# A flag over the softmax sums of a decode kernel, and a branch at the end to a second form of the layers

## The chip, the cores and the metric

The kernel runs on one core of one Trainium2 chip. The metric is the device time of one launch in microseconds (us), less is better. Every run is one whole launch: four decode layers, from the inputs in HBM to the output in HBM. The profile comes from one execution of its own, with its own time beside its span.

## What is computed

A token step for 8 batch rows (`x` is 8 x 1 x 448) passes through attention, mixer and MLP, and then through the same two again with the same weights and the same caches:

```python
def _A_ref(x, k_cache, v_cache, wq, wo):
    q = (x @ wq).reshape(B, 1, 16, 256).transpose(0, 2, 1, 3)
    k = jnp.repeat(k_cache, 2, axis=1)      # caches: 8 x 8 x 4096 x 256 bf16
    v = jnp.repeat(v_cache, 2, axis=1)
    p = softmax(einsum("bhqd,bhkd->bhqk", q, k) * 256 ** -0.5)
    return einsum("bhqk,bhkd->bhqd", p, v).transpose(0, 2, 1, 3).reshape(B, 1, 4096) @ wo

x = x + _A_ref(layernorm(x), k_cache, v_cache, wq, wo)
x = x + _B_ref(layernorm(x), w1, w2, w3, w4)     # twice, A then B
```

The sequence has one token, so the shifted groups of the mixer inside `_B_ref` are zero, and the kernel computes of B only the inner norm and the MLP (448 to 1792 to 448, tanh gelu). The softmax of the reference subtracts the row's maximum; the kernel takes exp of the scaled scores as they are, sums them, and divides at the end.

## The kernel before, in words

The keys and the values are 134 MB each over all rows, far more than the on-chip memory, so they stream. The work is cut into units of one pass (0 or 1, for the two attention layers), one batch row and one pair of key heads (`gp`, 4 of them). A unit has four chunks of K and four of V, of 1 MB each. Python lists fix the order by hand: `items` is the order of use, `loads` the order of the transfers, and `emit_loads` (L948) puts a load on SP's queue as soon as one of 17 places of 8,192 bytes per partition (`places`, L80) is given up by its last reader. Part of each row's K and V stays on the chip between the two passes. All transfers of the caches go through SP's one queue, and a waiting load holds up those behind it.

For a K chunk DVE turns 32 x 32 blocks (`transpose_k`, L1017), PE forms the scores (L1036), and ACT takes exp with a running sum (`exps`, L1044), whose sums land in `zall`. PE turns the weights p (L1087), ACT spreads them (L1286), and PE multiplies them with V (L1104, or L1120 for the last row).

`z_cols` (L521) runs 55 times, once for each group of units that is finished: DVE adds the two partial sums into `zs` (L527), spreads them over four columns (L530), PE adds over the partitions with a matrix of ones (L538), and DVE takes the reciprocal into `rz` (L541). `zs`, `zm` and `rz` have one buffer each. The instructions of such side work are generators, stepped between the chunks (`step`, L1190), so their place in every engine's queue is fixed when the program is built.

GpSimd (POOL) does little: it makes the identity matrix, and raises variances to the power -0.5 (L304 and, in the tail, L1572).

The tail begins with the last V chunks (L1120 and L462 in turn), and goes on with the sum over wo, the double norm (L1530 to L1576), the MLP (L1581, L1606, L1614, L1630), the last addition (L1639) and four small transfers of the output, two from SP and two from ACT (L1641). Behind them stands the end of the program (all under L1669): every engine goes on into the block that follows; SP waits for the eight DMA semaphores and the engines' counters, and two rounds of a barrier of all five engines close the run.

Small constants (`usel`, `parity`, `wv`, `one`, `eps2`, `nhalf`) are tiles of their own, behind `places` in the same pool.

Of the kernel before, what the change touches and what calls it, by code (L numbers as in the profile page):

```python
# [8 lines left out]
FP32 = mybir.dt.float32  # L9
BF16 = mybir.dt.bfloat16  # L10
U32 = mybir.dt.uint32
ACT = mybir.ActivationFunctionType
ALU = mybir.AluOpType
EPS = 1e-5


@with_exitstack
def kernel(
# [12 lines left out]
    out: bass.AP,  # L31
):

    nc = tc.nc
    Bn, Sq, D = A_x.shape
    G = A_k_cache.shape[1]
# [2 lines left out]
    HD = A_wq.shape[1]  # L51
# [43 lines left out]
    identb = consts.tile([128, 128], BF16, name="identb")  # L95
    nc.vector.tensor_copy(identb[:], ident)

    usel = consts.tile([128, 4], FP32, name="usel")
    for u in range(2):
        nc.vector.tensor_reduce(  # L100
            usel[:, 2 * u : 2 * u + 2],
# [2 lines left out]
            ALU.add,  # L104
        )

    parity = consts.tile([128, 2], FP32, name="parity")
    nc.vector.tensor_reduce(
        parity[:], ident.rearrange("p (m k) -> p k m", k=2), mybir.AxisListType.X, ALU.add
    )  # L110
    xq = consts.tile([128, 2, Bn], BF16, name="xq")

# [35 lines left out]
        at, n = {"y": (0, 8), "st": (64, 2)}[what]  # L148
        return store[0][:, at : at + n * nb]

    wv = consts.tile([128, 4], FP32, name="wv")
    nc.vector.memset(wv[:, 0:3], 1.0 / D)
    nc.vector.memset(wv[0:64, 3:4], 0.0)
    nc.vector.memset(wv[64:128, 3:4], 1.0 / D)
    one = consts.tile([128, 1], FP32, name="one")
    nc.vector.memset(one[:], 1.0)
    ones = one[:].to_broadcast([128, 128])
    HTw = consts.tile([128, HC, Bn], BF16, name="HTw")
    nc.vector.memset(HTw[:], 0.0)
    low = consts.tile([128, 2, 4], FP32, name="low")  # L160
    for k, v in enumerate((1.0, (1 + EPS) ** -0.5)):
        nc.vector.memset(low[:, k], v)
        nc.vector.memset(low[0:64, k, 3:4], 0.0)
    eps2 = consts.tile([128, 2], FP32, name="eps2")
    nc.vector.memset(eps2[:, 0:1], EPS)
    nc.vector.memset(eps2[:, 1:2], EPS * EPS / (1 + EPS))
    nhalf = consts.tile([128, 1], FP32, name="nhalf")
    nc.vector.memset(nhalf[:], -0.5)
    xb = {}
    for nb in (1, Bn):  # L170
        xb[nb] = consts.tile([128, 5, nb], BF16, name=f"xb{nb}")
# [72 lines left out]
    def norm(x, nb, twice, xe=None):  # L244

        xe = xbs(nb) if xe is None else xe

        def room(name, shape, at):  # L250
            n = shape[0] * shape[1]
            if nb < Bn:
                t = chn.tile([128, n * MID], FP32, tag=name)
                ap = t[:, 0 : n * nb]
            else:
                ap = scratch(at, n * nb)
            return ap.rearrange("p (s f b) -> p s f b", s=shape[0], f=shape[1])

        def bc(ap):
            return ap.unsqueeze(1).to_broadcast([128, 4, nb])  # L260

        xx = room("xx", (2, 4), 0)
        nc.vector.tensor_mul(xx[:, 0], x, wv[:].unsqueeze(2).to_broadcast([128, 4, nb]))
        nc.vector.tensor_mul(xx[:, 1], xx[:, 0], x)
        mv = room("mv", (1, 2), 528)[:, 0]
        if nb == 1:
            yield 3
            st = room_ps("st", 1)
            nc.tensor.matmul(
                st, ones, xx.rearrange("p s f b -> p (s f b)"), start=True, stop=True  # L270
            )
            yield 0
            nc.vector.tensor_reduce(
                mv[:, :, 0],
                st.rearrange("p (s f) -> p s f", s=2),
                mybir.AxisListType.X,
                ALU.add,
            )
        else:
            xs = room("xs", (1, 2), 512)[:, 0]  # L280
            nc.vector.tensor_reduce(
                xs, xx.rearrange("p s f b -> p s b f"), mybir.AxisListType.X, ALU.add
            )
            yield 3
            st = room_ps("st", nb)[:, 0 : 2 * nb].rearrange("p (s b) -> p s b", b=nb)
            nc.tensor.matmul(st, ones, xs, start=True, stop=True)
            yield 0
            nc.vector.tensor_copy(mv, st)
        var = room("var", (1, 1), 608)[:, 0, 0]
        if nb == 1:  # L290
            nc.vector.scalar_tensor_tensor(
                var, mv[:, 0], mv[:, 0], mv[:, 1], ALU.mult, ALU.subtract, reverse1=True
            )
        else:
            nc.vector.tensor_mul(var, mv[:, 0], mv[:, 0])
            nc.vector.tensor_sub(var, mv[:, 1], var)


        ve = room("ve", (1, 2), 544)[:, 0]
        n = 2 if twice else 1  # L300
        rs = room("rs", (1, 2), 560)[:, 0]

        def power(k0, k1):
            nc.gpsimd.tensor_tensor(  # L304
                rs[:, k0:k1].rearrange("p n b -> p (n b)"),
                ve[:, k0:k1].rearrange("p n b -> p (n b)"),
                nhalf[:].to_broadcast([128, (k1 - k0) * nb]),
                ALU.pow,
            )

        if twice and nb == 1:
            nc.vector.scalar_tensor_tensor(
                ve[:, :, 0], var.to_broadcast([128, 2]), 0.0, eps2[:], ALU.max, ALU.add
            )
            power(0, 2)
        else:
            if twice:
                nc.vector.tensor_scalar(
                    ve[:, 1], var, 0.0, EPS * EPS / (1 + EPS), ALU.max, ALU.add
                )  # L320
                power(1, 2)
            nc.vector.tensor_scalar(ve[:, 0], var, 0.0, EPS, ALU.max, ALU.add)
            power(0, 1)
        xc = room("xc", (1, 4), 576)[:, 0]
        nc.vector.tensor_tensor(xc, x, bc(mv[:, 0]), ALU.subtract)  # L325
        yield 0
        if nb > 1:
            yield
        c = (1 + EPS) ** -0.5 if twice else 1.0
        rl = rs[:, n - 1]  # L330
        parts = ((0, 128, 0, 0, 3, 0), (0, 64, 64, 3, 4, 4), (64, 128, 64, 3, 4, 3))
        if nb == 1:
            nc.vector.scalar_tensor_tensor(
                xe[:, 0:4, 0], xc[:, :, 0], rl, low[:, int(twice)], ALU.mult, ALU.mult
            )
            parts = parts[1:2]
        for p0, p1, x0, f0, f1, to in parts:
            pp = slice(x0, x0 + p1 - p0)
            dst = xe[p0:p1, to : to + f1 - f0, :]
            if nb == 1:  # L340
                nc.vector.tensor_scalar(dst, xc[pp, f0:f1], rl[pp], c, ALU.mult, ALU.mult)
            else:
                nc.vector.scalar_tensor_tensor(
                    dst,
                    xc[pp, f0:f1],
                    c,
                    rl[pp].unsqueeze(1).to_broadcast([p1 - p0, f1 - f0, nb]),
                    ALU.mult,
                    ALU.mult,
                )  # L350
        if twice and nb == 1:
            nc.vector.scalar_tensor_tensor(x, xc, rs[:, 0], x, ALU.mult, ALU.add)
        elif twice:
            nc.vector.tensor_tensor(xc, xc, bc(rs[:, 0]), ALU.mult)
            nc.vector.tensor_add(x, x, xc)
        yield 2
# [36 lines left out]
    def tail_cols(r0, r1, ps, two):  # L393

        nb = r1 - r0
        nc.vector.tensor_copy(
            two.rearrange("p (r k) -> p r k", k=2),
            identb[:, 64:128].unsqueeze(2).to_broadcast([128, 64, 2]),
        )
        nc.tensor.matmul(ps, two, xb[Bn][:, 3, r0:r1], start=True, stop=True)  # L400
        nc.vector.tensor_tensor(
            xq[:, :, 0:nb],
            ps.unsqueeze(1).to_broadcast([128, 2, nb]),
            parity[:].unsqueeze(2).to_broadcast([128, 2, nb]),
            ALU.mult,
        )
        return lambda xi: xb[Bn][:, xi, r0:r1] if xi < 3 else xq[:, xi - 3, 0:nb]
# [109 lines left out]
    def mlp(b0, nb):  # L517
        HT = yield from mlp_hidden(b0, nb)
        yield from out_cols(lambda c: HT[:, c, :], w4_of, range(HC), b0, nb, 2)

    def z_cols(zall, gps):  # L521

        np_ = len(gps)
        zm = chn.tile([128, 4, np_], FP32, tag=f"zm{np_}")
        zs_t = chn.tile([128, 2], FP32, tag="zs")
# [4 lines left out]
        nc.vector.tensor_tensor(  # L530
            zm[:],
            zs.unsqueeze(1).to_broadcast([128, 4, np_]),
            usel[:].unsqueeze(2).to_broadcast([128, 4, np_]),
            ALU.mult,
        )
        yield
# [2 lines left out]
        yield 0  # L539
        rz = chn.tile([128, 4, np_], FP32, tag=f"rz{np_}")  # L540
        nc.vector.reciprocal(rz[:], z_ps)  # L541
        return rz

    def scale_o(o_ps, rz, gp, u, OT):
# [746 lines left out]
    for idx, it in enumerate(items):  # L1291
        if idx == len(items) - 2:
# [6 lines left out]
            x_ps = store[1][:, 0:W]  # L1299
            nc.vector.memset(x_ps, 0.0)  # L1300
            nc.scalar.activation(end[1][:, W : W + 1], identb[:, 0:1], ACT.Gelu_apprx_tanh)
        n, kv, c = it
        ps, b, gp = tasks[n]
        if idx in o_late_at:
# [235 lines left out]
        return ap.unsqueeze(1).to_broadcast([ap.shape[0], n, nb])  # L1540

    xx = temp(8 * nb).rearrange("p (s f b) -> p s f b", s=2, f=4)
    nc.vector.tensor_mul(xx[:, 0], xs, wv[:].unsqueeze(2).to_broadcast([128, 4, nb]))
    nc.vector.tensor_mul(xx[:, 1], xx[:, 0], xs)
    m_ps = store[4][:, 256 : 256 + 8 * nb]
    nc.tensor.matmul(m_ps, ones, xx.rearrange("p s f b -> p (s f b)"), start=True, stop=True)
# [23 lines left out]
    nc.vector.tensor_scalar(ve[:, 0:nb], var, 0.0, EPS, ALU.max, ALU.add)  # L1570
    for k in (nb, 0):
        nc.gpsimd.tensor_tensor(  # L1572
            rs[:, k : k + nb], ve[:, k : k + nb], nhalf[:].to_broadcast([128, nb]), ALU.pow
        )
    centre(xe[0:64, 4:5, :], 64, 128, 3, 4)
    centre(xe[64:128, 3:4, :], 64, 128, 3, 4)  # L1576
# [66 lines left out]
        )  # L1643


# [1 line left out]
_INS = ['A_x', 'A_k_cache', 'A_v_cache', 'A_wq', 'A_wo', 'B_x', 'B_w1', 'B_w2', 'B_w3', 'B_w4']  # L1647
_OUTS = [((8, 1, 448), 'bfloat16')]
# [25 lines left out]
```

## Time and profile before

| | us |
|---|---|
| median of three runs | 1033.33 (1033.24 to 1033.99) |
| profiled execution, its own time | 1033.59 |
| its span (first to last instruction) | 1031.4 |
| outside the span | 2.2 |

| engine | busy us | share of the span | instructions |
|---|---|---|---|
| PE, matmul | 660.3 | 64% | 12706 |
| DVE | 585.0 | 57% | 1211 |
| ACT | 213.1 | 21% | 688 |
| POOL | 16.3 | 2% | 27 |
| SP's DMA queue, of 16 DMA engines | | 99.2% | 67840 packets, 419.66 MB |

How to read it: the span is one execution from its first instruction to the last barrier. A line such as L541 is a line of the kernel before; in the changed kernel the same statement has a higher number. "Idle before" is the time an engine stood still ahead of a group, and the name behind the arrow says who ended it. SPq, ACTq and so on are the engines' instruction queues, in which a DMA is issued. The part on the DMA queues counts what the 16 transfer engines did; q8 and q14 there carry the program itself to the engines.

### The profile page before, as it was taken

To read this page: it belongs to the slowest core of one execution; us is meant where nothing else is said; L and a number is where in the kernel's file an instruction comes from. 1 tells how busy PE (TensorE), PEld (TensorE's weight loads), DVE (VectorE), ACT (ScalarE), POOL (GpSimd) and SP (SyncE) were. 2 spreads that over 40 slices of the span, in tenths; PEclk is the share of its full clock that TensorE was granted. 3 is DMA by queue.
4 is the path that set the end of the run, shared out by engine and by line. 5 is a ranking of instruction groups with operands and counts; after the bars stand their busy time and mean duration, and the time that the engine had idled before them with its cause. 6 is when DMAs were issued, how large, how long until landed. Compare 5 with 4: busy or idle time off the path is not lost.

```text
span 1031.4 us, 28604 instructions
## 1 busy us (share of the span) xinstructions
PE 660.3 (64%) x12706; PEld 419.0 (41%) x12706; DVE 585.0 (57%) x1211; ACT 213.1 (21%) x688; POOL 16.3 (2%) x27
## 2 busy tenths in 40 slices
PE   2154545776578558765875587567765775577775
PEld 2032323453245335533553355334533453345545
DVE  6344577259725971596259725882497159625581
ACT  1011111141214120411141214121422041214120
POOL 0000000000000000000000000000000000000000
PEclk9965555565665665755565656556656575666655
DMA  9999999999999999999999999999999999999995
GB/s 377 394 428 420 422 425 418 401 409 424 415 404 423 423 415 402 414 424 414 397 418 422 417 406 418 423 417 401 415 424 414 407 412 425 417 395 419 416 421 209
DMA packets 68010, 421.48 MB, mean 409 GB/s; under 512 B 7080, under 2 KB 11952, under 8 KB 42288
## 3 DMA queue, kind: packets, MB, share of 16 engines
q1 hardware_dynamic: 67840, 419.66, 99.2%
q8 instruction: 99, 1.62, 0.6%
q14 instruction: 23, 0.19, 0.1%
q10 hardware_dynamic: 48, 0.01, 0.0%
HBM read 419.63 MB, written 0.01 MB: 407 GB/s over the span
## 4 chain that ended last, share of the span: by engine, by line
DMA 51%; DVE 22%; PE 20%; issue 3%; ACT 2%; SPq 1%; POOL 0%; DVEq 0%; ACTq 0%
DMA places<-in_A_v_cache_dram 35%; DVE places L1021 18%; DMA places<-in_A_k_cache_dram 14%; PE sc L1036 8%; PE o L1104 5%; PE misc L601 2%; PE misc L180 2%; DMA w_sb<-in_B_w_dram 1%; DVE qbd L424 1%; ACT p_n L1045 1%; PE misc L538 1%; SPq L199 1%; DVE store L1067 1%; PE misc L462 1%; PE misc L1087 1%
## 5 line engine op out<-in xcount | busy, mean ns | idle before, releaser
L1021 DVE STREAM_TRANSPOSE places<-places 128x512 uint32<-128x512 uint32 (+2 forms) x384 | 443.7, 1212 | 43.2 <-DMA places<-in_A_k_cache_dram 42.9
L1104 PE MATMUL o<-places,ptw 128*8 128x256 bf16 x3808 | 247.4, 383 | 141.7 <-DMA places<-in_A_v_cache_dram 113.1
L1036 PE MATMUL sc<-places,qbd 128*8 128x256 bf16 (+1 forms) x4736 | 234.5, 354 | 145.4 <-DVE places L1021 143.0
L1036 PEld LDWEIGHTS <-qbd 128*8 128x8 bf16 x4736 | 123.2, 105 | 211.4 <-DVE places L1021 122.7
L1104 PEld LDWEIGHTS <-ptw 128*8 128x8 bf16 x3968 | 102.9, 101 | 207.7 <-issue 130.4
L1045 ACT ACTIVATE p_n<-sc 128x256 bf16<-128x256 f32 x128 | 95.5, 746 | 326.8 <-PE sc L1036 323.3
L1286 ACT COPY ptw<-psv 128x32 bf16<-128x32 bf16 x248 | 52.9, 228 | 179.3 <-PE o L1104 177.5
L424 DVE CAST qbd<-misc 32x16 bf16<-32x16 f32 (+1 forms) x184 | 30.8, 168 | 62.2 <-PE misc L418 60.4
L601 PE MATMUL misc<-R_t,o_t 128*128 128x4 f32 (+1 forms) x212 | 46.3, 325 | 27.7 <-DVE qbd L424 11.3
L601 PEld LDWEIGHTS misc<-R_t,o_t 128*128 128x128 f32 x212 | 42.1, 276 | 44.4 <-issue 18.1
L1094 ACT CAST psv<-misc 128x128 bf16<-128x128 f32 x64 | 17.0, 266 | 196.3 <-PE misc L1087 196.3
L541 DVE RECIPROCAL rz<-misc 128x4 f32<-128x4 f32 (+1 forms) x55 | 9.4, 172 | 82.2 <-PE misc L538 37.9
L1072 ACT COPY places<-store 128x1024 bf16<-128x1024 bf16 x40 | 40.2, 1028 | 11.2 <-PE o L1104 10.9
L538 PE MATMUL misc<-zm,one 128*128 128x4 f32 (+1 forms) x110 | 28.3, 328 | 18.2 <-DVE zm L530 15.8
L538 PEld LDWEIGHTS misc<-zm,one 128*128 128x128 f32 x110 | 23.5, 266 | 33.7 <-DVE zm L530 22.1
L180 PEld LDWEIGHTS <-w_sb 128*128 128x128 bf16 x896 | 27.7, 105 | 16.5 <-issue 16.5
L1045 ACT ACTIVATION_READ_ACCUMULATOR p_n<-sc 128x1 f32 x128 | 34.0, 266 | 0.0
L555 ACT COPY o_t<-o 128x256 f32<-128x256 f32 x53 | 19.7, 372 | 58.2 <-PE o L1104 58.2
L304 POOL TENSOR_TENSOR t<-t,nhalf 128x2 f32<-128x2 f32 (+2 forms) x18 | 12.0, 669 | 951.4 <-DVE t L325 951.4
L1067 DVE TENSOR_SCALAR store<-places 128x512 uint32<-128x512 uint32 x40 | 24.8, 673 | 0.0
L1087 PEld LDWEIGHTS <-p_n 128*128 128x128 bf16 x256 | 11.5, 105 | 30.2 <-issue 19.3
L605 DVE CAST qT<-misc 128x8 bf16<-128x8 f32 (+1 forms) x37 | 7.2, 195 | 27.8 <-PE misc L601 20.1
(157 smaller groups left out, 370.7 us busy)
## 6 DMA issues: line engine op xcount, KB each, us to landing
places<-in_A_k_cache_dram SPq DMA_DIRECT2D x79, 2048.0 KB, 15.3
places<-in_A_v_cache_dram SPq DMA_DIRECT2D x193, 512.0 KB, 7.1
places<-in_A_v_cache_dram SPq DMA_DIRECT2D x87, 1024.0 KB, 19.5
places<-in_A_k_cache_dram SPq DMA_DIRECT2D x34, 1024.0 KB, 12.0
rest<-in_A_v_cache_dram SPq DMA_DIRECT2D x8, 640.0 KB, 16.3
places<-in_A_wq_dram SPq DMA_DIRECT2D x5, 768.0 KB, 12.8
places<-in_A_v_cache_dram SPq DMA_DIRECT2D x8, 384.0 KB, 15.7
wo_sb<-in_A_wo_dram SPq DMA_DIRECT2D x1, 2688.0 KB, 19.7
```

Of the source, the lines that this page charges most:

```text
L180: nc.tensor.matmul(bass.AP(out.tensor, out.offset, [out.ap[0], (1, WIDE)]), w, x.to_broadcast([128, WIDE]), start=start, stop=stop, skip_g ...
L424: nc.vector.tensor_copy(qbd[32 * a : 32 * a + 32, :, g0 : g0 + ng, a, :], qs.rearrange("p e (f g u h) -> p (e f) u g h", f=2, u=2, h=2)[:, ...
L538: nc.tensor.matmul(z_ps, ones, zm[:], start=True, stop=True)
L601: nc.tensor.matmul(ot_ps[:, j], o_sb[:].rearrange("p (i j) -> p j i", j=2)[:, j], R, start=True, stop=True)
L1021: nc.vector.transpose(w, w)
L1036: nc.tensor.matmul(sc[32 * k : 32 * k + 8, 128 * (x % 2) : 128 * (x % 2 + nx)], qbd[:, ep, gp % 2].rearrange("p a h -> p (a h)"), v, start ...
L1045: nc.scalar.activation(p_sb[:, :, :, 2 * u : 2 * u + 2].rearrange("p t i x -> p x t i"), sc[:, 0:256].rearrange("p (x t i) -> p x t i", x= ...
L1067: nc.vector.tensor_single_scalar(kept_words.bitcast(U32), words.bitcast(U32), 0, op=ALU.bitwise_or)
L1072: nc.scalar.copy(words, kept_words.bitcast(BF16))
L1087: nc.tensor.matmul(pt_ps[:, t], p_sb[:, t].rearrange("p i x -> p (i x)"), cols, start=True, stop=True,)
L1104: nc.tensor.matmul(o_ps[32 * q : 32 * q + 8, :], ptz[:, at : at + 8], v[:, y * Dh : (y + 1) * Dh] if v2 is None or y < PR else v2[:, (y - ...
L1286: nc.scalar.copy(ptw[:, ring_of[it], :, 6:8], psv[slot_of[it[0]]][:, it[2]])
```

## The change

The old body becomes a function `layers_unshifted`. Each call of `z_cols` now adds its reciprocals and its sums into a tile `seen` on POOL: two additions per call, 110 in all. Before the last item of the list the sums of `seen` are added over the partitions (one matmul with ones), copied by ACT, added up by DVE and compared with 1e12: `bad` is 1 where the total is larger or not a number. At the end each engine loads `bad` into a register and branches. Where `bad` is 0, the engine goes on through a short block to the end; where it is 1, it runs `layers_shifted`, a second, plain form of all four layers, which subtracts the maximum ahead of exp and writes the output again. The second form stands in the program between the branch and the end.

In the built program this gives each engine a register load and a compare-and-branch behind its last instruction (SP's register load stands ahead of its two output transfers). In the short block for `bad` = 0 every engine waits for its own counter and raises it by what the other way would have added; SP does so for the eight DMA semaphores, one wait each, and then all jump over the second form: over 17,619 instructions on PE, 1,910 on DVE, 522 on SP, 275 on ACT and 21 on POOL, of 64 bytes each. In the closing block SP has eight waits instead of five ahead of the barriers. In the first form the engines' instructions keep their order; what is new among them are POOL's additions, the four instructions of the flag, and a wait for POOL at the addition into `zs` on DVE, since POOL must have read the last `zs`.

The small constants become parts of one tile `few`, and `seen` and `bad` are placed first. In the lists of tile addresses of the two built programs `places` begins at byte 16,512 of each partition before and at byte 16,608 after (remainders by 64: 0 and 32; by 256: 128 and 224), `rest` moves likewise, and the kept weights go the other way: `wq_sb` from 163,616 to 163,584 (remainders by 64: 32 and 0), and `w3_sb`, `wo_sb` and `w4_sb` with it.

```diff
+SAFE = 1e12
...
+    flags = ctx.enter_context(tc.tile_pool(name="flags", bufs=1))
+    seen = flags.tile([128, 12], FP32, name="seen")
+    bad = flags.tile([128, 1], mybir.dt.int32, name="bad")
+    layers_unshifted(tc, seen[:], bad[:], A_x, ..., out)
+    flag = tc.nc.values_load(bad[0:1, 0:1], min_val=0, max_val=1)
+    with tc.If(flag > 0, preferred_fallthrough_block=False):
+        layers_shifted(tc, A_x, ..., out)
...
+    few = consts.tile([128, 16], FP32, name="few")
+    def small(n):
+        ...
+        return few[:, at : at + n]
+    nc.gpsimd.memset(seen, 0.0)
-    usel = consts.tile([128, 4], FP32, name="usel")
+    usel = small(4)
...
     def z_cols(zall, gps):
...
         rz = chn.tile([128, 4, np_], FP32, tag=f"rz{np_}")
         nc.vector.reciprocal(rz[:], z_ps)
+        for e, part in (
+            (seen[:, 0 : 4 * np_], rz[:].rearrange("p n g -> p (n g)")),
+            (seen[:, 8 : 8 + np_], zs),
+        ):
+            nc.gpsimd.tensor_tensor(e, e, part, ALU.add)
         return rz
...
+        if idx == len(items) - 1:
+            seen_ps = store[4][:, 0:2]
+            nc.tensor.matmul(seen_ps, ones, seen[:, 8:10], start=True, stop=True)
+            nc.scalar.copy(seen[:, 8:10], seen_ps)
+            nc.vector.tensor_reduce(
+                seen[:, 10:11], seen[:, 0:10], mybir.AxisListType.X, ALU.add
+            )
+            nc.vector.tensor_scalar(bad, seen[:, 10:11], SAFE, 0.0, ALU.is_le, ALU.is_equal)
...
+def layers_shifted(ctx, tc, A_x, ..., out):
+    for _ in range(2):
...
+        for b in range(Bn):
+            for g in range(G):
+                kt = work.tile([128, NS, Dh], BF16, name="kt")
+                nc.sync.dma_start(kt[:], A_k_cache[b, g].rearrange("(p n) d -> p n d", p=128))
+                vt = work.tile([128, NS, Dh], BF16, name="vt")
+                nc.sync.dma_start(vt[:], A_v_cache[b, g].rearrange("(p n) d -> p n d", p=128))
...
+                    nc.scalar.activation(p[:, h], s[:, h], ACT.Exp, bias=down[:, h : h + 1],
+                                         accum_out=z[:, h : h + 1])
...
+    nc.sync.dma_start(out.rearrange("b s d -> (b s) d"), rows[:])
```

## The prediction

> **What bounds the kernel now.** I read the page's DMA rows first, then the end of the chain of waits and the timeline there, then SP's waits, then the packet records of the trace, then POOL's rows.
>
> ```profile
> DMA  9999999999999999999999999999999999999995
> GB/s 377 394 428 420 422 425 418 401 409 424 415 404 423 423 415 402 414 424 414 397 418 422 417 406 418 423 417 401 415 424 414 407 412 425 417 395 419 416 421 209
> ...
> q1 hardware_dynamic: 67840, 419.66, 99.2%
> q8 instruction: 99, 1.62, 0.6%
> q14 instruction: 23, 0.19, 0.1%
> ```
>
> The 16 transfer engines are busy from the first slice to the last but one: the bytes on SP's queue are the bound, not an engine. In the packet records a packet of the caches takes about 8 ns plus 0.0369 ns per byte (medians 159 ns for 4,096 bytes, 312 for 8,192, 613 for 16,384). Summed by that line, the packets make 1,001 us of the 1,021 us up to the last V packet. The missing 20 us are hiccups of less than a microsecond.
>
> The chain of waits at the end, and the timeline of its last lines:
>
> ```profile
> 1006.18 15.25 DMA places<-in_A_v_cache_dram
> 1021.42 0.05 issue
> 1021.47 0.39 PE store L1120 x8
> 1021.86 0.02 issue
> 1021.88 0.18 DVE qT L548
> ...
> 1028.29 0.27 DVE places L1639
> ```
>
> ```profile
> 1028.29 0.27 DVE L1639 TENSOR_TENSOR places<-places,store 128x112 bf16<-128x112 f32 x1
> 1028.59 0.71 SPq L1641 DMA_DIRECT2D out_dram<-places  x2
> 1028.60 0.65 ACTq L1641 DMA_DIRECT2D out_dram<-places  x2
> ```
>
> From 1021.4 on nothing is transferred: one chain of small steps runs to 1028.56, then the output goes out. SP's waits in that window:
>
> ```profile
> SPq L1641 <- DVE places L1639: 17.4, 1, 17.4
> SPq L1669 <- DMA out_dram<-places: 1.1, 1, 1.1
> SPq L1669 <- PEq L1669: 0.6, 2, 0.4
> ```
>
> SP's issue ends at 1029.30; 1.1 us later, at 1030.40, the output has landed. The other 1.04 us to 1031.44 are SP's further waits (each starts 0.065 us after the one before) and the two barriers. So two places count: the stream, where only what reaches the transfers costs, and the 10 us after it, where everything on the chain costs in full.
>
> **The change part by part.**
>
> *In the stream.* POOL gets 110 additions of 128x1 to 128x8. No plain addition on POOL is in the trace; the nearest rows:
>
> ```profile
> L304 POOL TENSOR_TENSOR t<-t,nhalf 128x2 f32<-128x2 f32 x8 | 5.6, 701 | 824.3 <-DVE t L325 824.3
> L304 POOL TENSOR_TENSOR t<-t,nhalf 128x1 f32<-128x1 f32 x8 | 4.4, 551 | 78.8 <-DVE t L325 78.8
> L304 POOL TENSOR_TENSOR t<-t,nhalf 128x4 f32<-128x4 f32 x2 | 2.0, 1012 | 48.3 <-DVE t L325 48.3
> ...
> L1658 POOL MEMSET const-float32-0.0<- 128x1 f32 x1 | 0.1, 98 | 0.2 <-issue 0.2
> ```
>
> A power is the dearest thing POOL does here, a fill the cheapest, so one addition costs between 0.1 and 0.55 (one column) or 1.0 us (four); by 55 pairs that is 11 to 85 us on an engine busy for 16.3 of 1031. Behind POOL's queue stand only its own powers: each starts 6.4 us or more after the reciprocal ahead of it, and a pair needs at most 1.7 us with its hand-overs of 0.05 to 0.07. Cost nothing.
>
> DVE's addition into `zs` now waits until POOL has read the last `zs`. In the trace it follows the previous reciprocal by 1.01 to 1.45 us eleven times and by 4.06 us or more otherwise. A pair at 0.3 us each is done in 0.7, a pair of powers in 1.7; so it waits 0 to 0.7 us, eleven times at most, 0 to 7 us on DVE. Queued behind it are the transposes (L1021), for which PE's scores wait, and through the places SP's loads. I take nothing: the loads are 7 to 20 us from issue to landing, and the transfer engines stay at 1.01 in the densest DVE stretch (217 to 250 us, DVE busy 27.4 of 33). If that cover is gone, the few hiccups near these waits (0.6 us at 207, 0.2 at 412) say about 0.3 us for each of eight places: up to 2.4 us.
>
> Could POOL slow DVE by reading on-chip memory at the same time? At 969.03 three transposes ran beside two powers with two inputs each, and took 1235, 667 and 668 ns; without POOL the same forms take 1180 to 1240 and 660 to 680. Nothing.
>
> *In the tail.* The matmul with ones (and its loads) stands on PE between two V chunks. Row: L538 at 1014.86 took 0.57 us. PE finishes the chunk ahead at 1019.95 and starts the next at 1020.19, when it lands; now it starts near 1020.6, and its two pieces end near 1021.6, where the last 8 matmuls would have begun at 1021.47. Bounds 0 and 0.4; I take **0.2**, since the last piece still waits for its transfer. ACT's copy (idle until 1026.46) and DVE's two instructions (about 0.15 each) end near 1021.4, ahead of DVE's next step at 1021.88; hidden, and 0.3 us if that half microsecond of cover is gone. SP's register load waits for them with 7 us until the output.
>
> *At the end.* In the order of SP: the output lands at 1030.40 + 0.2. Eight waits in the short block instead of the first of five: the three for the output end with the landing, six more at 0.065 make 0.4, the branch 0.05. Then the jump, F. Then eight waits in the closing block, where four were left: 0.26 more. Together **0.7 + F**. ACT comes beside it: its issue ends at 1029.25, a register load (not in the trace; between 0.05 for an instruction that the sequencer does alone and the 2.1 us that the load of x takes from issue at 0.73 to its use at 2.85) ends by 1031.35, so at worst it adds 0.5. Nothing taken.
>
> F is the largest term. In the trace each branch goes to the next block, and DVE enters the closing block about 0.05 us after its last instruction is handed over. Now the target lies 522 x 64 = 33,408 bytes ahead on SP and 1.13 MB on PE. The program comes in packets: 99 of 16,384 bytes on q8, which is PE's 24,945 instructions of 64 bytes in order, and 23 of 8,192 bytes on q14 for the others. They come one block after the other in order, so the target cannot be there and has to be fetched while the engine stands. Price from rows: issue to first packet, as for the output (1028.59 to 1029.38), 0.79; the packet, 1.06 on q8 and 0.32 on q14; last packet to the wait's end (1029.80 to 1030.40), 0.60. That is 1.7 us for SP's block and 2.45 for PE's. PE is there by 1028.2 plus a register load of at most 2.1, so it ends near 1032.8, much like SP at 1032.7. Lower bound 0.05, upper bound two such fetches in series, 4.9. I take **2.45**, the dearer of the two single fetches, since the barrier waits for the last of five engines.
>
> [...]
>
> *Start.* POOL's clearing of `seen` is one more 0.1 us beside a stream that SP starts at 0.73; `few` changes no count. Nothing.
>
> Sum: 0.2 + 0.7 + 2.45 = 3.35 us on the execution of 1033.59, which lies 0.26 above the median shown; on the median **1036.7 us**, 0.32% slower.
>
> **The rivals.**
>
> *The jump is cheap* (not slower than a measurement tells). If the target is at hand, or the engines fetch it while SP waits for the landing, F is 0.05 and the end costs 0.2 + 0.75: **1034.3**. For it: PE, DVE and ACT do wait up to 2 us for SP in any case, and the fetch packets are short. Against it: SP itself jumps after the landing. It decides if F stays under 1.2 us.
>
> *The places lie worse.* `places` moves from remainder 0 by 64 bytes to 32. In the packet records, without those held up by over 12%, 4,096-byte packets of wq took 163.8 ns into `wq_sb` (remainder 32), V's of that size 161.5 into `places` (remainder 0); 1,792-byte ones 78.5 into the kept weights, 76.1 into `places`. If these 2.4 ns belong to the address, some 57,300 packets of the stream pay them on 16 engines: 8.6 us, less 0.5 for 3,456 packets of weights that get better: 8.1 more, **1044.8**. Against it: the 896-byte packets go to remainder 32 as well and have a median of 41.0, exactly the line, and the first packets into `wo_sb` take 74, the line too; a toll of the address would spare none. So the difference looks like crowding in that stretch.
>
> [...]
>
> *POOL reaches the transfers* through the wait on `zs`: 2.4 more, **1039.1**.
>
> *The change does something else:* the flag comes out as 1, and the second form runs. Its caches alone, 537 MB at 409 GB/s, are 1,313 us more, over **2340**. The sums are of some 4,096 terms near 1 for each head, the total far from 1e12.
>
> **How the numbers follow.** Forecast (1035.4 to 1039) 0.58; cheap jump 0.14; places worse 0.17, at the second price 0.03; POOL 0.06; second form 0.01; anything faster 0.01. A measurement of this kernel tells about 0.2%, 2.1 us, from no change. Faster 0.01, same 0.14, slower 0.85. The range goes from just under the cheap jump, 1034.2, to just over the first price of the address, 1045; outside are the second price, the second form and little else.
>
> **What would show it.** In the changed profile: the first output packet 0.2 us later, and between the landing and the span's end some 4.2 us instead of 1.04, with instruction packets in them; cache packets at the same 159, 312 and 613 ns and 99% busy; rows of POOL's additions under 0.5 us, and no wait for POOL ahead of L1021. I am wrong if the gap behind the landing stays under 2 us (F), if the medians of the packets move by 2 ns or more (address), or if SP's waits for DVE grow (POOL).

## The result, and the profile after

| | before | after |
|---|---|---|
| median | 1033.53 us (1033.24 to 1034.45) | 1041.07 us (1039.20 to 1042.13, six runs) |
| profiled execution, its own time | 1033.59 | 1039.20 |
| its span | 1031.44 | 1037.41 |

The changed kernel is slower: ratio 1.0069, 95% interval 1.0056 to 1.0082. It costs 7.5 us where 3.35 were forecast. The time lies in the range, 4.4 us above the forecast; it lies above the 1035.4 to 1039 that the forecast itself stood for, and the range reaches so far only because it was drawn out to the rival of the address. The profiled execution happens to be the fastest of the six, so its parts add up to 5.6 us and not to 7.5.

The page of the changed kernel, DMA rows:

```profile
DMA  9999999999999999999999999999999999999993
GB/s 381 410 425 420 420 423 415 399 423 423 412 400 425 425 409 391 414 424 411 402 417 425 411 403 420 424 412 392 424 422 406 402 417 423 411 392 414 419 419 148
...
q1 hardware_dynamic: 67840, 419.66, 98.7%
q8 instruction: 101, 1.65, 0.6%
q14 instruction: 31, 0.25, 0.1%
```

SP's queue carries the same 419.66 MB, so the second form did not run. The program comes in 2 packets more on q8 and 8 more on q14. Two and six of them come behind 1031 us, when the engines jump; the other two on q14 also come in `watch_only` and `near` below, which have no far jump. The last slice has fallen from 209 to 148 GB/s, since it holds more time without transfers.

Its chain of waits at the end (start, us, what):

```profile
1007.63 15.86 DMA places<-in_A_v_cache_dram
1023.49 0.05 issue
1023.53 0.39 PE store L1153 x8
1023.92 0.02 issue
1023.95 0.18 DVE qT L581
...
1030.43 0.27 DVE places L1681
```

The steps shown are those of before, 2.1 us later from 1023.49 on. Its timeline, first at the new matmul, then at the output:

```profile
1021.80 0.56 PE L1338 MATMUL store<-seen,few 128*128 128x2 f32 x2
1022.21 0.51 PEld L1153 LDWEIGHTS <-places 128*128 128x128 bf16 x16
1022.22 1.03 PE L1153 MATMUL store<-psv,places 128*128 128x2 bf16 x24
...
1023.53 0.38 PE L1153 MATMUL store<-psv,places 128*128 128x2 bf16 x8 [0.28 <-DMA places<-in_A_v_cache_dram]
...
1030.73 0.70 SPq L1683 DMA_DIRECT2D out_dram<-places  x2
1030.73 0.65 ACTq L1683 DMA_DIRECT2D out_dram<-places  x2
```

Ahead of its last 8 matmuls PE still waits 0.28 us for the last piece of V (0.26 before), so the new matmul delays nothing there. SP's waits behind 1020 us (total, times, longest):

```profile
SPq L39 <- DVE bad L1343: 15.0, 1, 15.0
SPq L1683 <- DVE places L1681: 6.9, 1, 6.9
SPq L40 <- SPq L40: 1.3, 3, 0.7
SPq L1892 <- PEq L1892: 0.6, 2, 0.4
```

SP waits 15 us for the flag (L39), but the output needs 6.9 more: hidden. The three waits of L40 are the output's landing. Between them and L1892, the closing block, no row shows anything: the branch instructions are counted in no view, so that gap has to be read from the sequencer's records in the trace. There SP's last branch starts at 1033.23 and its next instruction at 1036.08.

Cut into four stretches that join, both profiled executions read so (last packet of the weights, last packet of V, first issue of the output, end of the span):

| us | before | after | difference |
|---|---|---|---|
| start to the end of the weights | 51.23 | 49.90 | -1.33 |
| stream, weights to last V packet | 969.77 | 973.07 | +3.30 |
| tail, last V packet to output issue | 7.60 | 7.75 | +0.15 |
| end, output issue to end of span | 2.85 | 6.67 | +3.82 |
| outside the span | 2.15 | 1.79 | -0.36 |

So two places changed: the end, as forecast, and the stream, which the forecast had at nothing.

### The profile page after: what moved, and what is told of

The parts are those of the page before. It is cut to its first block, busy times and chain, and to the rows that moved or that the text cites. A ratio compares the mean times of both kernels' runs of the same rounds, so it can differ in the third digit from the quotient of the medians.

```text
span 1037.4 us, 28804 instructions
## 1 busy us (share of the span) xinstructions
PE 660.3 (64%) x12708; PEld 417.4 (40%) x12708; DVE 585.7 (56%) x1213; ACT 213.3 (21%) x689; POOL 35.4 (3%) x138
## 3 DMA queue, kind: packets, MB, share of 16 engines
q1 hardware_dynamic: 67840, 419.66, 98.7%
## 4 chain that ended last, share of the span: by engine, by line
DMA 48%; DVE 24%; PE 20%; issue 4%; ACT 2%; SPq 1%; POOL 0%; DVEq 0%; ACTq 0%; POOLq 0%
DMA places<-in_A_v_cache_dram 36%; DVE places L1054 18%; DMA places<-in_A_k_cache_dram 11%; PE sc L1069 8%; PE o L1137 5%; PE misc L634 2%; PE misc L205 2%; DVE store L1100 2%; DVE qbd L449 1%; DMA w_sb<-in_B_w_dram 1%; PE misc L566 1%; SPq L224 1%; ACT p_n L1078 1%; PE misc L487 1%; DVE rz L569 1%
## 5 line engine op out<-in xcount | busy, mean ns | idle before, releaser
L1069 PE MATMUL sc<-places,qbd 128*8 128x256 bf16 (+1 forms) x4736 | 237.1, 355 | 149.3 <-DVE places L1054 147.9
L566 PE MATMUL misc<-zm,few 128*128 128x4 f32 (+1 forms) x110 | 28.6, 331 | 19.2 <-DVE zm L558 16.8
L574 POOL TENSOR_TENSOR seen<-seen,rz 128x4 f32<-128x4 f32 (+1 forms) x55 | 11.1, 202 | 842.2 <-DVE rz L569 813.1
L566 PEld LDWEIGHTS misc<-zm,few 128*128 128x128 f32 x110 | 23.8, 269 | 35.0 <-DVE zm L558 23.3
```

Of the source, the lines that this page charges most:

```text
L566: nc.tensor.matmul(z_ps, ones, zm[:], start=True, stop=True)
L1069: nc.tensor.matmul(sc[32 * k : 32 * k + 8, 128 * (x % 2) : 128 * (x % 2 + nx)], qbd[:, ep, gp % 2].rearrange("p a h -> p (a h)"), v, start ...
```

## The experiments

Theory at the start: the stretch at the end is the fetch behind the far jump, and the stream is the address of `places`. Rivals: the additions on POOL or the longer program slow the stream; the flag's loads and the barrier make the end, at any distance.

**1. The address alone, `addr96`.** The kernel before, with its places where the change puts them:

```diff
+    consts.tile([128, 24], FP32, name="pad")
     places_t = consts.tile([128, NC * PB], BF16, name="places")
...
-    usel = consts.tile([128, 4], FP32, name="usel")
+    few = consts.tile([128, 16], FP32, name="few")
+    usel = small(4)
```

> The kernel before with the places of the buffers after and nothing else: the small constants in one tile, and an unused tile of 96 bytes ahead of the places, which begin at byte 16,608 (remainder 32 by 64) while the kept weights begin at 163,584 (remainder 0). No flag, no additions on POOL, no branch. The changed kernel is 7.5 us slower in the median; 3.8 of that are behind the last transfers and 0.2 in the tail, so some 3.5 us should be in the stream. Address theory: all of these come from the remainder, 1036 to 1038 us, cache packets of 8,192 and 16,384 bytes with medians near 313 and 614 ns, weight packets all on the line (140, 74). POOL theory (the additions and their wait hold up the loads): no slower than before, 1032.5 to 1033.7. Program theory (the longer program or its place in HBM disturbs the stream): the same 1032.5 to 1033.7.

Measured: 1035.98 us beside 1033.34, ratio 1.0026 (1.0016 to 1.0035). Stream 972.95, weights done at 50.74, end 2.84. The stream's +3.2 are there without any of the change's instructions.

**2. The change without the address, `after64`.** The flag becomes a slice of `seen`, which moves the places to 16,576, 0 by 64 as before:

```diff
-    seen = flags.tile([128, 12], FP32, name="seen")
-    bad = flags.tile([128, 1], mybir.dt.int32, name="bad")
+    seen = flags.tile([128, 16], FP32, name="seen")
+    bad = seen[:, 12:13].bitcast(mybir.dt.int32)
```

> The changed kernel with the flag's word inside the tile of the sums, so that 64 instead of 96 bytes stand ahead of the places: they begin at 16,576, remainder 0 by 64, and the kept weights at remainder 32, as before the change. Everything else is as changed. Address theory: the 3.5 us of the stream go, 1036.8 to 1038 us, cache packets back at medians of 312 and 613 ns or less. POOL theory and program theory: no change, 1040 to 1042.

Measured: 1038.05 us, 1.0052 (1.0038 to 1.0066). Stream 970.45, tail 7.74, end 6.45. The time lies 0.05 above what the address theory said and 2 us below its rivals. By the medians the address gives 2.6 and the rest of the change 4.7, together 7.3 of the 7.5.

**3. Watching alone, `watch_only`.** The sums and the flag stay, at the change's addresses:

```diff
-    flag = tc.nc.values_load(bad[0:1, 0:1], min_val=0, max_val=1)
-    with tc.If(flag > 0, preferred_fallthrough_block=False):
-        layers_shifted(tc, A_x, ..., out)
```

> The changed kernel without the register loads, the branch and the second form; the additions on POOL, the total and its comparison stay, and so do the addresses. The end should fall back to 2.85 us from the output's issue to the span's end (6.68 after). Address theory and POOL theory: 1037 to 1038 us (the stream stays slow). Program theory: the program is as short as before, so the stream recovers too, 1033.5 to 1034.2.

Measured: 1036.29 us, 1.0027 (1.0017 to 1.0038), 0.3 us from `addr96`, well inside the intervals; stream 973.21, end 2.85. The 110 additions cost nothing that can be measured. In the changed kernel they read (count, then busy us, mean ns, idle before):

```profile
L574 POOL TENSOR_TENSOR seen<-seen,rz 128x4 f32<-128x4 f32 x46 | 9.3, 202 | 654.4 <-DVE rz L569 625.2 <-DVE R_t L617 29.1
L574 POOL TENSOR_TENSOR seen<-seen,zs_t 128x1 f32<-128x1 f32 x46 | 8.8, 191 | 0.0
```

0.2 us each, and SP's largest wait hardly moved. Over the whole run, before:

```profile
SPq L929 <- DVE places L1021: 158.4, 30, 16.0
```

and in the changed kernel:

```profile
SPq L962 <- DVE places L1054: 159.1, 29, 16.4
```

The POOL rival falls. So does the rival of the longer program: without the second form the stream is as slow as with it (973.21 and 973.07).

**4. The same branch over a short block, `near`.** `layers_shifted` is cut to its last transfer and one load ahead of it:

```diff
 def layers_shifted(...):
     rows = keep.tile([Bn, D], BF16, name="rows_s")
     nc.sync.dma_start(rows[:], A_x.rearrange("b s d -> (b s) d"))
-    ...
     nc.sync.dma_start(out.rearrange("b s d -> (b s) d"), rows[:])
```

> The changed kernel with the second form cut down to two small transfers, so that it leaves out the second way of computing; the branch is there and its target lies some 30 instructions ahead. If the jump over the long form costs 2.8 us on SP and 3.6 on PE because the target has to be fetched, the end falls from 6.68 to about 4 us and the run to 1038 to 1039 us under the address or the POOL theory, 1034.5 to 1035.5 under the program theory. If the cost lies in the branch itself and not in the distance, the end stays at 6.7 us and the run at 1040 to 1042.

Measured: 1035.82 us, 1.0024 (1.0014 to 1.0033), with the change's addresses. End 2.97. SP's waits behind 1005 us:

```profile
SPq L1735 <- DMA out_dram<-places: 0.6, 3, 0.3
SPq L1735 <- PEq L1735: 0.6, 2, 0.5
```

The output's landing is now waited for in the closing block (L1735): SP jumps while the output is under way, and its first wait there starts 0.37 us after the branch did. Register loads, branch and barrier are all in this kernel, and the end is 0.12 us longer than before; I had expected some 4 us. It differs from the changed kernel in more than the distance: its short block has two waits on SP in place of eight, and none for the output. So the other 3.7 us of the end are read from the sequencer's records of both. SP's far jump is 2.85 of them; the six waits behind the landing in the short block are 0.42, the way from there to the span's end is 0.17 longer (1.33 us behind the jump, 1.16 here behind the landing), and the output landed 0.27 later (2.08 us from issue, 1.81 here and before), for a reason that no run shows.

After these four I read the stream as a toll on places that are not 0 by 64. The next two runs were to confirm it, and they did not.

**5. Places and weights both 0 by 64, `all64`.** As `addr96` without the unused tile, and `few` of 24 columns.

> The kernel before with its five small constants as slices of one tile of 24 columns, so that the cache places (16,512) and the 32 weight places (163,520 and on) both leave 0 by 64; nothing else is changed. Address theory: the cache packets keep 159, 312 and 613 ns, and the weights fall from 146.1 and 79.0 ns (packets of 3,584 and 1,792 bytes, places that leave 32) to 140.0 and 74.2, as in the two profiles in which their places left 0; there the weights were done 0.5 to 1.3 us earlier. So 1032.2 to 1033.0 beside 1033.4 for the kernel before. Rival (the packets of the weights are short for another reason, or the stream behind them gives it back): 1033.4 within 0.3.

Measured: 1033.02 us beside 1033.51, 0.9996 (0.9987 to 1.0005). The weights' packets took 144.9 and 79.0 ns, not 140.0 and 74.2, and the weights were done at 51.55. What the fast weights had in common was another thing: at 163,584 they leave 0 by 256; here they leave 192.

**6. Places 0 by 256, `addr128`.** As `addr96`, with 128 unused bytes ahead:

```diff
+    consts.tile([128, 32], FP32, name="pad")
     places_t = consts.tile([128, NC * PB], BF16, name="places")
```

> The kernel before with the five small constants in one tile of 16 columns and an unused tile of 128 bytes ahead of the pool, so that the cache places lie at 16,640 (0 by 64 and 0 by 256, where before they left 128 by 256) and the weight places leave 32 by 64 as before. If the remainder by 64 is all that counts: packets 159, 312, 613, time as before within 0.3 (1033.1 to 1033.7). [...]

Measured: **1022.29 us**, 0.9890 (0.9875 to 0.9906): 11 us faster than the kernel before, by 128 unused bytes (`few` itself gave nothing in 5). Stream 958.87. One row of the stretches view says it: 60 to 1,000 us, busy us (instructions) of PE, its weight loads, DVE, ACT and POOL, then PE's clock, DMA share, GB/s. Before:

```profile
60.00:1000.00 940.00, 625.20 (x11888) 392.46 (x11884) 550.87 (x1100) 202.79 (x661) 12.00 (x18) 0.59 1.01 415
```

and `addr128`:

```profile
60.00:1000.00 940.00, 626.93 (x12070) 395.35 (x12067) 554.37 (x1109) 203.01 (x664) 12.01 (x18) 0.61 1.01 420
```

The share of the transfer engines is the same 1.01, the bytes go at 420 GB/s in place of 415. "Busy" does not tell an engine that moves bytes from one that pays for where they go. In the packet records the 8,192-byte packets behind the weights read (10th, 50th, 90th percentile): 309, 309, 309 ns in `addr128`; 309, 312, 319 before; 309, 313, 320 after. On a place with remainder 0 at least eight packets in ten take the same time; on the others some packets pay.

**7. A remainder of 32, `rem32`.** Does the toll follow the bytes between the multiple of 256 below and the packet's start? Small tiles move ahead of the places:

```diff
+    few = consts.tile([128, 16], FP32, name="few")
+    fold = consts.tile([128, 8], FP32, name="fold")
+    xq = consts.tile([128, 2, Bn], BF16, name="xq")
+    low = consts.tile([128, 2, 4], FP32, name="low")
     places_t = consts.tile([128, NC * PB], BF16, name="places")
```

> The kernel before with small tiles moved ahead of the cache places, so that these lie at 16,672 (32 by 256) and the weights leave 32 as before. So far the stream behind the weights took 958.9 us with remainder 0, 969.8 and 969.3 with 128, 970.5 to 971.3 with 192 and 972.7 to 973.2 with 224. [...] Theory of the bytes between the line of 256 below and the packet's start: 224 over 128 cost 3.3 us for 96 bytes, so 32 would be 3.3 us below 128: stream 966.5, time 1030.1, and the step from 32 to 0 would be 7.6 us. Were it the remainder by 64 after all (32 against 0), it would be as slow as 224: 972.7, and 1036.0.

Measured: 1037.32 us beside 1033.24, 1.0039 (1.0026 to 1.0052); stream 972.74. 32 is as slow as 224, so the number of these bytes sets no price. (The whole time is 1.3 us above `addr96`; 0.85 of it lies ahead of the stream, where the weights on 32 are done at 51.59 in place of 50.74.) The row of its stretch shows the rate:

```profile
60.00:1000.00 940.00, 618.71 (x11867) 387.05 (x11863) 549.73 (x1099) 201.22 (x658) 12.01 (x18) 0.61 1.01 414
```

**8. A remainder of 0 by 512, `rem512`.** `few`, `fold`, `xq` and `identb` stand ahead of the places, which begin at 16,896.

> The kernel before with small tiles moved ahead of the cache places, so that these lie at 16,896, which leaves 0 by 512 (at 16,640, the fast place, they left 256); the weights leave 32 by 256 as before. If 256 bytes is the step that counts: as with 16,640, 1022.3 within 0.5, packets with medians 309 and 611. If it is 512 or more: a second step, below 1019 where it is as large as the first.

Measured: 1022.35 us, 0.9895 (0.9881 to 0.9909); stream 957.26. No second step: 256 is enough. So the stream has three levels:

| places by 256 | kernels | stream behind the weights, us |
|---|---|---|
| 0 | addr128, rem512, best256, change256 | 957.3 to 959.7 |
| 128 or 192 | before, all64, after64 and its two variants below | 969.3 to 971.3 |
| 32 or 224 | after, addr96, watch_only, near, rem32 | 972.7 to 973.2 |

**9. The branch the other way round, `after64_other`.** Experiment 2 with one word changed:

```diff
-    with tc.If(flag > 0, preferred_fallthrough_block=False):
+    with tc.If(flag > 0, preferred_fallthrough_block=True):
```

> The changed kernel with the cache places back at 16,576 (0 by 64), and with the branch the other way round: the block behind the branch falls through to the second form and the taken jump goes to the end (the flag given to the branch as likely). Theory of the fetch: the end is long because the jump reaches code that was not fetched; with this order SP jumps before it waits for the output to land, so that the fetch of 2.8 us lies beside the 1.8 us of landing. The stretch from output issue to span end falls from 6.45 us to 4.4 to 5.2, and the time from 1038.05 to 1036.0 to 1037.0. Rival (the fetch is held up by the landing, or all five engines meet again at the far block and the last of them sets it): 6.2 to 6.9 us and 1037.8 to 1038.4.

Measured: 1037.62 us beside 1033.51, 1.0044 (1.0031 to 1.0058); end 5.67 in place of 6.45. SP's waits behind 1005 us:

```profile
SPq L40 <- SPq L40: 2.9, 1, 2.9
SPq L1892 <- PEq L1892: 0.6, 2, 0.4
```

The order did what it should: SP branches at 1030.56, right behind its issue, and the 2.9 us of its fetch (in which the output lands) show as one wait. Between the two theories' numbers in size: 1.64 us of landing and waits are no longer ahead of the jump, but the fetch took 0.24 longer (2.97 against 2.73), and the eight waits of the short block, which were part of those 1.64, now stand behind it with 0.63. By the times, 0.4 us, the intervals of 2 and 9 do not separate.

**10. A hint ahead of the branch, `after64_hint`.**

```diff
+    tc.mark_branch_hint_location("skip")
     flag = tc.nc.values_load(bad[0:1, 0:1], min_val=0, max_val=1)
-    with tc.If(flag > 0, preferred_fallthrough_block=True):
+    with tc.If(flag > 0, preferred_fallthrough_block=True, label="skip"):
```

> The kernel of the run with the branch the other way round, with a hint instruction ahead of the load of the flag that names the branch and its likely target. If the hint has the target's code fetched ahead of the jump: output issue to span end near the 2.97 us of the kernel whose second form is two transfers, and 1034.0 to 1035.2. If the hint does nothing on this chip: as that other run, within 0.3. If it costs by itself: above it, by the durations of the hint instructions in the trace.

Measured: 1037.21 us, 1.0034 (1.0022 to 1.0046); end 5.56. SP's next instruction starts 2.86 us after its branch (2.97 in 9). As written here the hint does not bring the target in ahead of the jump; a gain of 0.1 to 0.4 us over 9 cannot be told from none. The trace keeps no record of a hint instruction, so whether an engine carried one out is not shown.

**11. The fast addresses for the kernel before, `best256`.** `few`, `fold` and `xq` ahead of the places (16,640), and 96 unused bytes ahead of the weights (163,584).

> The kernel before with the five small constants, fold and xq moved ahead of the cache places (16,640) and 96 unused bytes ahead of the weights (163,584), so that both leave 0 by 256; nothing else. By the remainder of 256: weights' packets 140.0 and 74.2 ns as in the two profiles in which they left 0 (145 and 79 with 32, 192 and 224), the weights done some 0.5 us earlier, the stream as with 16,640: 1021.3 to 1022.2. If the weights' packets do not matter at the end: 1022.3 within 0.3.

Measured: **1021.36 us**, 0.9877 (0.9863 to 0.9892), the fastest kernel of this study. Weights' packets 140.0 and 74.0 ns, done at 50.45.

**12. The fast addresses for the change, `change256`.** Experiment 2 with `few` ahead of the places and 32 unused bytes ahead of the weights, which gives the same two addresses.

> The changed kernel (watching, loads of the flag, branch, whole second form, order of the branch as in the change) with cache places at 16,640 and weights at 163,584, both 0 by 256: its flag is a slice of seen, few stands ahead of the places, and 32 unused bytes ahead of the weights. Theory: with places alike the change costs its tail (0.15) and its end (6.45 to 6.67 us from output issue to span end in place of 2.85, less 0.4 outside the span): 3.3 to 3.6 us in a profiled execution over the unchanged kernel with the same places, and up to 4.7 in the timed ones, so 1024.8 to 1026.7, below the kernel before by 7 to 8. Rival (the sums by GpSimd or the longer program cost something that the worse places hid): over 1028.

Measured: 1024.98 us, 0.9920 (0.9906 to 0.9934): with all its watching and its branch, below the kernel before. Stream 959.72, tail 7.73, end 6.18. Its stretch:

```profile
60.00:1000.00 940.00, 624.26 (x12055) 393.97 (x12054) 554.23 (x1107) 203.54 (x664) 30.48 (x126) 0.61 1.01 420
```

POOL's 18 us more (30.48 against 12.01) stand beside the same 420 GB/s. At equal addresses the change costs 3.6 us, by the medians of 11 and 12 as by their profiled executions (1025.33 and 1021.74): end +3.34, tail +0.29, stream +0.97, weights -0.62, outside the span -0.37. The stream's part is no more than the four streams at this remainder differ (957.3 to 959.7).

## Why the forecast was right in sign and too small

**Tail, forecast 0.2: right in size, not by its path.** 0.15 in the changed kernel, 0.08 in `watch_only`, 0.29 in 12 against 11. The new matmul took 0.56 us (row of before: 0.57) and ran between two chunks, but PE then waited for the last piece of V as before, so the matmul was hidden; where the 0.15 arises no run shows. That the size came out is luck.

**End, forecast 0.7 + 2.45 = 3.15: right in kind, 0.7 too small.** Measured +3.82. The mechanism holds: SP waits for the output, waits on, and then stands at the far jump. In the changed kernel these are 0.27 for an output that landed later, 0.42 for six waits, 2.85 from the branch to the next instruction and 0.29 for the longer closing block, 3.83 together; the same branch over a short block (`near`) costs 0.12 in all. The 0.7 of waits and branch was sized well. What was mis-sized is F, and its path was another. The sequencer's records of the changed kernel, from each engine's branch over the second form to its next instruction:

| engine | jumps over, instructions | branch starts, us | next instruction, us | between |
|---|---|---|---|---|
| POOL | 21 | 1029.29 | 1029.45 | 0.16 |
| PE | 17,619 | 1030.56 | 1034.20 | 3.64 |
| DVE | 1,910 | 1031.29 | 1034.25 | 2.95 |
| ACT | 275 | 1032.23 | 1034.87 | 2.64 |
| SP | 522 | 1033.23 | 1036.08 | 2.85 |

I took PE's fetch as the dearest and therefore the one that counts. It is the dearest, but PE jumps 2.67 us ahead of SP; SP jumps last, since it first waits for the output, and the barrier waits for SP. SP's fetch: 1.21 us to a packet of 8,192 bytes at 1034.44, 0.31 for it, 1.33 from there to the next instruction. (The packets of q14 do not name their engine; I go by the order, in which three of them follow the jumps of DVE, ACT and SP by 1.06, 0.95 and 1.21 us.) The forecast priced these at 0.79, 0.32 and 0.60 from the output's transfer, 1.7 in all; here a landed transfer released a wait in 0.60 us, and SP's next instruction came only 1.33 behind its packet. So F was 2.8 on SP where the forecast had 1.7 for SP and took PE's 2.45. The other 0.3 us: the output was 2.08 us from issue to the last of its landing waits, not 1.81. Register loads took 0.48 to 0.56 us, all beside other work. The 0.36 us that the span's surroundings lost were in no step; every kernel here with a branch has 1.79 to 1.88 outside the span, every one without 2.15 to 2.26. That an engine stands at a far jump was an estimate in the forecast, from how the packets of the program come in the trace of before; in the table a jump over 21 instructions cost 0.16 us, and jumps over 275 and more cost 2.6 to 3.6.

**Stream, forecast nothing: wrong.** This is the step that failed. The forecast put the new addresses at nothing; they cost 2.6 us by the medians of experiment 1. In the profiled pair it is +3.30 in the stream and -1.33 at the weights, 2.0; in the profile of `addr96`, with the same addresses, +3.18 and -0.49, 2.7. (The two kernels with the long second form and the weights on 0 have these done 0.6 to 0.9 us earlier than those with the same addresses and no far jump, 49.83 and 49.90 against 50.45 to 50.77; no run explains it.) One sign that I had set for being wrong did come: the median of the 4,096-byte packets moved by 2 ns, from 159 to 161 over the whole run. The address was the rival "the places lie worse", with a price of 8.1, three times too much, and neither what was set against it nor the comparison it was worked out from holds:

- "A toll of the address would spare none." It spares many: the fastest tenth of the 8,192-byte packets takes 309 ns on 0, 128 and 224 by 256 alike, and the medians of 4,096, 8,192 and 16,384 bytes moved by 2, 1 and 1 ns only. The toll lies in the slower part of the packets, which I had set down as hiccups. The line of 8 ns plus 0.0369 per byte lies within 2 ns of the packets that do not pay (159, 309, 611).
- The comparison of `wq_sb` with `places`, 2.4 ns apart, could not show the step. Both stood on remainders that pay (32 and 128 by 256), and none of the packets of 3,584 bytes or more of the kernel before began on 0. Nor were `wq_sb`'s 163.8 ns the price of its own address: with `wq_sb` still on 32 and the places on 0 (`addr128`, `rem512`) the same packets took 159.0. Over the packets of V (4,096 bytes, those held up left out) the address is worth 0.5 ns (161.5 before, 162.0 after), not the 2.4 between `wq_sb` and `places`.

Measured, a place on 0 by 256 saves 3 ns a packet on average (10.9 us x 16 engines over some 57,300 packets), much the same at each size (means of `addr128` and before: 162.9 and 165.6, 311.7 and 315.5, 615.4 and 618.4), and one on 32 or 224 costs some 0.9 more than one on 128 or 192 (3.3 us by the same working). The weights' packets of 3,584 bytes have both steps: 140.0 ns on 0, 144.9 on 192, 145.9 to 146.1 on 32 and 224. So the runs show a step between 0 by 256 and the other remainders that were run, for writes into on-chip memory. It is no toll on every packet: half of the 4,096-byte packets take 159 ns on 128 as on 0. No run shows the second price of the address that the chances and the range of the forecast name; what the runs show in its place is that 32 and 224 by 256 cost the same (stream 972.74 and 972.7 to 973.2 us).

**POOL and DVE, forecast nothing: right** (experiments 3 and 12).

**Sum.** Forecast 3.35; with equal addresses 3.6 was measured (11 and 12), and 4.7 by the medians of experiment 2, whose places are on the same level as before. So that part was 0.3 to 1.4 too small, with a fetch too cheap and a surrounding that got shorter. The address adds 2.6.

**Open.** The six runs of the changed kernel spread over 2.9 us and the five of `after64` over 3.6, those of `addr96` over 1.1; of the changed kernel and of `after64` the profiled run is the fastest. I would look for it in the fetch, which varied from 2.5 to 3.0 us on SP in five profiles, but no trace of a slow one was caught. Nor did any run show which packets pay on an unaligned place, or by what mechanism the two steps arise, from 0 to 128 or 192 and from there to 32 or 224.

## What to carry to other kernels

When a change adds or moves small tiles, compare the addresses of the large transfer targets by 256 before and after, in kernels bound by transfers above all: here two tiles of together 52 bytes, which moved the places by 96, cost 2.6 us, and a deliberate move of 128 bytes gave 11. The branch over a long rare block cost a code fetch of 2.5 to 3.0 us on the engine that jumps last. A short block made it 0.12 us at the end in all; letting that engine jump before its last wait took 0.8 us off the end in one profile, which the times do not confirm. A row that lacks a case cannot speak against it: ask first whether the trace holds the situation at all.

## What the hardware did that I had not expected

- Transfer engines at a busy share of 1.01 can still gain 1.2%: 415 GB/s became 420 by the place's remainder alone.
- On places that leave 0 by 256, packets of one size take one time: the 10th and the 90th percentile agree for 4,096, 8,192 and 16,384 bytes (159, 309, 611 ns).
- From the end of the code packet behind SP's jump to SP's next instruction 1.33 us passed, more than the 0.6 us from the output's last packet to the end of the wait for it.
- A plain addition on POOL took 0.19 to 0.20 us at 1 to 8 columns, where a power takes 0.55 us at one and 1.64 at eight.
